# Regrouping y and z by batch: VectorE transposes in place of SBUF copies, in a linear-attention and spectral-mixing kernel

## The chip, the cores and the metric

The kernel runs on one core of a Trainium2 chip. The metric is the device time of one execution in microseconds (us). The core has TensorE (PE), VectorE (DVE), ScalarE (ACT), GpSimd (POOL) and SyncE (SP), which run side by side and wait for one another through semaphores; each takes its instructions in order. SP and POOL also issue DMA transfers, which sixteen DMA engines carry out.

## The reference

An attention with a feature map feeds a spectral mixing layer. Batch is 8, heads 8, sequence 576, head dimension 64; the model width is 512 and 64 Fourier modes are kept.

```python
q_p, k_p = (phi(q), phi(k))                       # exp(+-(x w_phi - max|x w_phi|))
kv = np.einsum('bhsf,bhsd->bhfd', k_p, v)
z = np.sum(k_p, axis=2)
x = num / den                                     # q_p kv / (q_p z + 1e-6), heads side by side
X = np.fft.rfft(x, axis=1)                        # first 64 modes
Yr = einsum('bmd,mde->bme', Xr, w_r) - einsum('bmd,mde->bme', Xi, w_i)
Yi = einsum('bmd,mde->bme', Xr, w_i) + einsum('bmd,mde->bme', Xi, w_r)
y = np.fft.irfft(Y, n=S, axis=1)
u = x + y
out = u + np.maximum(u @ w_ch, 0.0)
```

The weights w_r and w_i have 64 x 512 x 512 float32 values each, 64 MB each, and each is used once.

## The kernel before, in words

The model width is cut into four groups g of 128 rows (two heads each), and the 64 modes into eight *octets* o of eight modes. A weight tile is (g, 2 o + i): one octet, one group, i = 0 for w_r and 1 for w_i; 64 tiles of 1 MB in bf16. They stream from HBM in one fixed order (`order`), issued by POOL (`wload`, `next_w`), converted to bf16 on the way, into a pool `pw` of nine slots. The last eight tiles are those of octets 6 and 7 for g = 2 and 3.

**Unit loop.** 16 units (a group and a pair of batches, `bp`) run through a software pipeline: features, kv, numerators, the normalised x into `xs`, and its forward Fourier transform (`freq`, `keep_x`) into `XT`. In between, `some(n)` takes n weight tiles from `mixq` and *mixes* each: eight matmuls of 512 columns on TensorE (`mix`). The sum over groups lives in `yacc`, one slot of 128x512 float32 for each octet. At the end of the loop, in the pass after the last unit, three mixes are done.

**Late stage.** Then the loop `while mixq` mixes the rest: a mix, then n *fills* from the list `todo`, the number dealt out evenly over the mixes that are left. `left` is the number of tiles still to be mixed. `todo` holds, in this order: 36 chunks of channel work (`Channels`: transpose x on TensorE, copy to `xT` on VectorE, multiply with w_ch, copy to `xw` on ScalarE; `hold(i)` turns chunk i + 1 ahead of the product of chunk i), in whose first entries the inverse Fourier tables CI, CL, CM are built (`inverse_tables`, on VectorE and ScalarE); then the *sums* (`Absorb`): the inverse transform of y is added to x on VectorE and that of z = y w_ch to xw on ScalarE or GpSimd. The fills are dealt so that at `left == 8`, which is when tile (3, 11) was mixed, all but the last channel chunks are done; the sums run between the last eight mixes.

**One octet.** When an octet is summed over all groups (its last mix has g = 3 and i = 1), VectorE forms `yst` (128 partitions, 512 bf16), TensorE transposes it, VectorE and ScalarE copy that to `yT`, TensorE multiplies by w_ch, and the result is `zst`. In `yst` and `zst` a partition is a mode, a part and a batch together, and the columns are e. The sums need the modes on partitions and the batch in the columns. This regrouping is done by `put`, one DMA from SP for each of y and z of octets 0 to 6, into 16 partitions of `yall` and `zall`, which with `yl` are three of the nine slots of `pw`; row 16 o + r holds octet o. The sums then use the first 96 rows (112 for the six chunks that are summed last, `early`), as six (seven) octets are there. Octets 6 and 7 go to `yl` too, for the last pairs of chunks (`Pair`), which sum them with the table CL, or straight from `yst` and `zst` with CM.

**Tail.** The last mix completes octet 7. Behind it follow the 18 pairs of chunks: sums, the rectifier, the addition and the stores to HBM.

Each engine's order is the program's order, fixed by `InOrder`; nothing is rescheduled. Operations are recorded through that helper, so that the profile gives nearly all of them as line 37; the tile names tell them apart.

Of the kernel before, what the change touches and what calls it, by code (L numbers as in the profile page):

```python
# [19 lines left out]
DMODEL = 512  # L20
# [23 lines left out]
def kernel(  # L44
# [470 lines left out]
    for n in range(-2, len(units) + 1):  # L515
        P, Q, K, R = (unit(n + i) for i in (-1, 0, 1, 2))
        X = 0 if n < 4 else 6 if n == 4 else 3
        if Q:
            Q.exp_q(0)
        if K:  # L520
            K.rows_k(0)
            K.exp_k(0)
        if Q:
            Q.weigh_v2()
            if n + 3 == len(units):
                unit(n + 2).load_v_parts()
            elif unit(n + 2):
                unit(n + 2).load_v()
        if P:
            P.freq()  # L530
            assert not any(key[0] == P.g - 2 for key in mixq)
            P.keep_x()
            if P.bp == NP - 1:
                mixq += [key for key in order if key[0] == P.g and (P.g < 2 or key[1] < 12)]
        if Q:
            Q.cols_q(1)
            Q.exp_q(1)
        some(1 if X else 0)
        if K:
            K.rows_k(1)  # L540
            K.exp_k(1)
        if Q:
            Q.kv()
        some(2 if n == 4 else 0)
        if K:
            K.rows_q(0)
            K.rows_k(2)
            K.rows_q(2)
            K.rows_q(1)
        if Q:  # L550
            Q.cols_q(2)
            Q.keep_kv()
            Q.exp_q(2)
        if K:
            K.exp_k(2)
            K.weigh_v()
        some(1 if X else 0)
        if R:
            R.turn_k(0)
        if K:  # L560
            K.shift_q()
        if R:
            R.turn_k(1)
        if Q:
            Q.num(0)
        if K:
# [12 lines left out]
        some(X - 2 + (n == 12))  # L579
        if n == -1:  # L580
            forward_table()
        if n < 3:
            next_w((2, 3, 2, 3, 2)[n + 2])
        elif n == 3:
            next_w(1)
        if n == 6:
            pool.dma_start(wchb, moe_w_ch.rearrange("(dc p) e -> p dc e", p=128))
    mixq += order[-8:]
    pm_cm.__exit__(None, None, None)
    pin_cm.__exit__(None, None, None)  # L590
# [53 lines left out]
    def inverse_tables():  # L644

        flat = xw[:, NP - 1].rearrange("p n e -> p (n e)").bitcast(F32)
        tok, ang, rnd = (flat[:, 640 * i:640 * i + 640] for i in range(3))
        small = pb.tile([128, 40], F32, name="small", bufs=1)
        dve.tensor_copy(eye, ident_b)
        ints = pb.tile([128, 16], I32, name="ints", bufs=1)  # L650
        for c in range(4):
            for a in range(2):
                dve.tensor_scalar_add(
                    out=tok[:, 128 * c:128 * c + 128].rearrange("k (p a) -> k a p", a=2)[:, a],
                    in0=nine, scalar1=float(4 * a + c))
        for i in range(2):
            dve.tensor_scalar_add(out=tok[:, 512 + 64 * i:576 + 64 * i], in0=nine, scalar1=8.0)
        used = [0, 0]
        yield

        def bits(src, shift, mask):
            t, f = ints[:, used[0]:used[0] + 1], small[:, used[1]:used[1] + 1]
            used[0] += 1
            used[1] += 1
            dve.tensor_scalar(out=t, in0=src, scalar1=shift, scalar2=mask,
                              op0=ALU.logical_shift_right, op1=ALU.bitwise_and)
            dve.tensor_copy(f, t)
# [10 lines left out]
        mode = calc(bits(pi, 4, 7), 8.0, jt)  # L678
        late = calc(calc(bits(pi, 4, 1), 8.0, 48.0), 1.0, jt)
        jm, tm, rm, b = bits(pi, 5, 3), bits(pi, 4, 1), bits(pi, 3, 1), bits(pi, 0, 7)  # L680
        last = calc(calc(tm, 4.0, jm), 1.0, 56.0)
        only = [calc(b, float(i), 1.0, ALU.is_equal, ALU.mult) for i in range(2)]
        yield
        for dst, m, r in ((CI, mode, r), (CL, late, r), (CM, last, rm)):
# [24 lines left out]
            yield  # L709
# [118 lines left out]

    def fill(n):
        for _ in range(n):  # L830
            if todo:
                todo.pop(0)()

    def put(src, o, dst, copies):
        if o < 7:
            sp.dma_start(dst[16 * o:16 * o + 16], src)
        if o > 5:
            for s in copies:
                r = 32 * s + 16 * (o - 6)
                (pool if o == 6 or s == 3 else sp).dma_start(yl[r:r + 16], src)  # L840
# [113 lines left out]
    while mixq:  # L954
# [3 lines left out]
            next_w(1)  # L958
        if not mixq:
            assert not todo  # L960
            pe.matmul(pys[o], lhsT=eye, rhs=yacc[:, o, :], start=False, stop=False)
# [10 lines left out]
        if g == NG - 1 and i == 1:  # L972
# [8 lines left out]
            else:  # L981
                for h in range(2):
                    dve.tensor_tensor(out=yst[:, H * h:H * h + H], in0=py[:, H * h:H * h + H],
                                      in1=yacc[:, o, H * h:H * h + H], op=ALU.add)
            put(yst, o, yall, (0, 2))
            if o < 5:
                fill(min(n, 1))
            for h in range(2):
# [14 lines left out]
            for e in range(2):  # L1003
# [13 lines left out]
            put(zst, o, zall, (1, 3))  # L1017
            fill(max(n - 2, 0) if o < 5 else n)
        else:
            fill(n)  # L1020
# [34 lines left out]
```

## Time and profile before

| | |
|---|---|
| three runs | 437.73, 438.81, 440.0 us; median 438.81 |
| profiled execution: span from first to last instruction | 436.2 us |
| busy: PE, DVE, ACT, POOL | 328.4, 293.7, 290.3, 118.9 us |
| mean granted TensorE clock | 0.906 |
| HBM read, written | 163.64 MB, 9.44 MB |
| weight tiles, issue to landing (median) | 27.8 and 28.9 us |

The profiled execution's own time is known as its span; the median of the runs lies 2.6 us above it, which is what lies around the span, and the difference between runs.

In the lines of the profile, `out<-in` are tile names, a bracket at the end gives how long the engine had been idle before and who released it, and "x8" joins eight instructions in a row. Matmuls overlap: one of 512 columns is shown with 0.38 us, but starts 0.22 after the one before. VectorE's instructions overlap in the same way: 0.68 long, 0.60 apart.

### The profile page before, as it was taken

What the parts mean: (1) busy time and instruction counts of PE and PEld (TensorE: products, weight loads), DVE (VectorE), ACT (ScalarE), POOL (GpSimd) and SP (SyncE); (2) the same over time, 40 slices, a digit from 0 to 9 for tenths busy, and PEclk for the clock granted to TensorE, in tenths of its full rate; (3) what the DMA queues carried; (4) which work ended last, traced back from release to release, by engine and by line L of the source; (5) the groups of instructions that cost most, each with busy time, mean ns of one, the idle gap of its engine ahead of it and who ended that gap; (6) DMA issues with size and microseconds to landing.
All of it is one profiled execution on the core that took longest, in us unless ns stands there. A gap on an engine that the chain in (4) does not pass through costs nothing.

```text
span 436.2 us, 10104 instructions
## 1 busy us (share of the span) xinstructions
PE 328.4 (75%) x4205; PEld 196.4 (45%) x4205; DVE 293.7 (67%) x583; ACT 290.3 (67%) x472; POOL 118.9 (27%) x157
## 2 busy tenths in 40 slices
PE   1567667778697686787796877934679999998992
PEld 1345555555465454554564554611334554333320
DVE  6768687665786777887877778722783333885794
ACT  3788697786887977986977778600444442665871
POOL 6232132113221212222222121211101111483790
PEclk9779898789998989998987998875899999999998
DMA  9999999999999999999999999999999999998697
GB/s 213 209 211 210 238 212 237 235 215 241 235 211 239 218 230 238 238 210 239 223 225 238 211 258 215 213 211 212 212 215 223 219 224 222 212 218 182 232 391 293
DMA packets 51896, 99.55 MB, mean 228 GB/s; under 512 B 2538, under 2 KB 13546, under 8 KB 51850
## 3 DMA queue, kind: packets, MB, share of 16 engines
q0 software_dynamic: 45136, 85.40, 100.1%
q1 hardware_dynamic: 6554, 13.44, 8.7%
q8 instruction: 33, 0.54, 0.5%
q14 instruction: 13, 0.11, 0.1%
q10 hardware_dynamic: 160, 0.07, 0.1%
HBM read 163.64 MB, written 9.44 MB: 397 GB/s over the span
## 4 chain that ended last, share of the span: by engine, by line
ACT 28%; PE 25%; DMA 24%; DVE 12%; issue 7%; POOL 2%; DVEq 0%; POOLq 0%; ACTq 0%
DMA wt<-in_moe_w_r_dram 16%; PE one L37 13%; ACT AQ L37 13%; ACT AB L37 9%; PE two L37 8%; DMA wt<-in_moe_w_i_dram 8%; DVE m L37 6%; ACT qT L37 3%; ACT XT L37 3%; PE pp L37 2%; DVE mk L37 2%; PE pt L37 2%; DVE xs L37 1%; DVE yacc L37 1%; DVE of L37 1%
## 5 line engine op out<-in xcount | busy, mean ns | idle before, releaser
L37 ACT ACTIVATE AQ<-two 128x1024 bf16<-128x1024 f32 x64 | 80.5, 1347 | 2.9 <-PE two L37 2.8
L37 ACT ACTIVATE AB<-two 128x1024 bf16<-128x1024 f32 x64 | 62.9, 1058 | 2.9 <-DVE mk L37 2.7
L37 ACT CAST xw<-pt 128x512 bf16<-128x512 f32 x50 | 29.4, 587 | 48.0 <-PE pt L37 48.0
L37 DVE TENSOR_REDUCE m<-two 128x8 f32<-128x1024 f32 x32 | 39.1, 1223 | 20.8 <-PE two L37 20.8
L37 POOL DMA_DIRECT2D wt<-in_moe_w_i_dram x28 | 20.9, 748 | 95.2 <-PE pt L37 37.6
L37 DVE TENSOR_REDUCE mk<-two 128x8 f32<-128x1024 f32 x32 | 38.9, 1218 | 8.6 <-PE two L37 8.6
L37 PE MATMUL two<-w2blk,qT 128*128 128x256 bf16 x128 | 22.3, 303 | 27.1 <-ACT AQ L37 14.8
L37 DVE TENSOR_TENSOR va<-vn,ee 128x1152 bf16<-128x1152 f32 x32 | 42.0, 1354 | 0.0
L37 PE MATMUL pt<-wchb,xT 128*128 128x512 bf16 x136 | 36.8, 395 | 6.6 <-DVE xT L37 5.5
L37 POOL DMA_DIRECT2D wt<-in_moe_w_r_dram x30 | 22.3, 744 | 63.3 <-PE one L37 27.0
L37 PEld LDWEIGHTS <-xs 128*128 128x128 bf16 x624 | 31.6, 103 | 12.2 <-issue 6.4
L37 PE MATMUL one<-wt,XT 128*32 128x512 bf16 x304 | 27.3, 446 | 10.4 <-DMA wt<-in_moe_w_i_dram 4.6
L37 ACT COPY qT<-one 128x512 bf16<-128x512 bf16 (+1 forms) x32 | 19.0, 642 | 24.3 <-PE one L37 24.3
L37 PE MATMUL two<-qT,w2blk 128*128 128x512 bf16 x64 | 27.8, 435 | 9.5 <-ACT AQ L37 9.5
L37 PEld LDWEIGHTS <-qT 128*128 128x128 bf16 x144 | 14.7, 103 | 41.8 <-issue 38.6
L37 PEld LDWEIGHTS <-XT 128*32 128x32 bf16 x512 | 14.7, 149 | 34.9 <-issue 24.2
L37 PEld LDWEIGHTS <-AQ 128*128 128x128 bf16 x512 | 24.5, 108 | 7.6 <-issue 4.1
L37 DVE TENSOR_TENSOR xs<-one,rd 128x384 bf16<-128x384 f32 x48 | 26.8, 557 | 1.6
L37 PE MATMUL one<-kvz,AQ 128*128 128x65 bf16 x512 | 27.1, 208 | 0.9 <-ACT qT L37 0.8
L37 PE MATMUL two<-mT,minus 96*128 96x512 bf16 x64 | 27.8, 434 | 0.0
L37 POOL DMA_DIRECT2D kb<-in_k_dram x16 | 11.4, 712 | 58.2 <-PE one L37 52.0
L37 DVE COPY xT<-pt 128x512 bf16<-128x512 bf16 x36 | 15.2, 421 | 17.5 <-PE pt L37 17.5
(142 smaller groups left out, 711.7 us busy)
## 6 DMA issues: line engine op xcount, KB each, us to landing
wt<-in_moe_w_r_dram POOLq DMA_DIRECT2D x30, 1024.0 KB, 27.8
wt<-in_moe_w_i_dram POOLq DMA_DIRECT2D x28, 1024.0 KB, 28.9
out_dram<-of SPq DMA_DIRECT2D x15, 512.0 KB, 3.5
vn<-in_v_dram POOLq DMA_DIRECT2D x13, 576.0 KB, 25.0
kb<-in_k_dram POOLq DMA_DIRECT2D x16, 288.0 KB, 20.4
qb<-in_q_dram POOLq DMA_DIRECT2D x16, 288.0 KB, 19.2
xs<-in_moe_w_i_dram POOLq DMA_DIRECT2D x2, 1024.0 KB, 23.6
out_dram<-of SPq DMA_DIRECT2D x6, 256.0 KB, 2.9
```

The lines of the kernel that those rows point to most:

```text
L37: ins = f(*args, **kwargs)
```

## The change

The 14 DMA copies of `put` go (its copies to `yl` stay). In their place each octet 0 to 6 is *parked*: `park` is a VectorE transpose of 32x32 blocks of 4-byte words, from `yst` (or `zst`) into the octet's slot of `yacc`, which is no longer needed by then. And `lay(bp)` regroups, with two more transposes of 128x512 words, the slots of all octets into the columns of `yall` and `zall` of one pair of batches. At octet 5 `lay(3)` and `lay(0)` are called; 1 and 2 follow in `fill`, when a sum that needs them is near; `lay(0)` is called again at octet 6. A pair of bf16 values moves as one word.

So that all eight slots hold something finite, octets 6 and 7 of `yacc` are copied to a new tile `late` by ScalarE and set to zero by GpSimd; the adds and the float32 matmul that used them read `late`. The sums use all 128 rows. The table CI follows the new order of rows.

`yall`, `zall` and `yl` take their slots of `pw` later: at `left` 11, 10 and 6, and at the first two no tile is issued. In the last pass of the unit loop one tile is mixed and not three; two are left to the late stage.

```diff
@@ unit loop @@
-        some(1 if X else 0)
+        some(1 if X and not end else 0)
...
-        some(X - 2 + (n == 12))
+        some(0 if end else X - 2 + (n == 12))
@@ late stage @@
-    zall = pw.tile([128, B_, DMODEL], BF16, name="zall", tag="wt")
-    yall = pw.tile([128, B_, DMODEL], BF16, name="yall", tag="wt")
-    yl = pw.tile([128, B_, DMODEL], BF16, name="yl", tag="wt")
+    late = pb.tile([128, 2, DMODEL], F32, name="late", bufs=1)
+    act.copy(late, yacc[:, 6:8, :])
+    pool.memset(yacc[:, 6:8, :], 0.0)
+    slots = yacc.bitcast(I32)
...
-            self.rows = slice(0, 112 if self.early else 96)
+            self.rows = slice(0, 128)
...
     def fill(n):
         for _ in range(n):
+            for f in todo[:4] if laid else ():
+                c = getattr(f, "__self__", None)
+                if isinstance(c, Absorb) and c.bp not in laid:
+                    lay(c.bp)
...
-    def put(src, o, dst, copies):
-        if o < 7:
-            sp.dma_start(dst[16 * o:16 * o + 16], src)
+    def park(src, o, z):
+        dve.transpose(
+            out=slots[:, o, 256 * z:256 * z + 256].rearrange("p (b k x) -> p k x b", b=8, k=8),
+            in_=src.bitcast(I32).rearrange("p (k x b) -> p k x b", k=8, b=8))
+    def lay(bp):
+        for z, dst in enumerate((yall, zall)):
+            dve.transpose(
+                out=dst[:, 2 * bp:2 * bp + 2].rearrange("p b e -> p (b e)").bitcast(I32).rearrange(
+                    "p (c o x) -> p c o x", o=8, x=4),
+                in_=slots[:, :, 256 * z + 64 * bp:256 * z + 64 * bp + 64].rearrange(
+                    "p o (c x) -> p c o x", x=4))
+        laid.append(bp)
...
-        next_w(1)
         left = len(mixq)
+        if left == 11:
+            yall = pw.tile([128, B_, DMODEL], BF16, name="yall", tag="wt")
+        elif left == 10:
+            zall = pw.tile([128, B_, DMODEL], BF16, name="zall", tag="wt")
+        else:
+            next_w(1)
+        if left == 6:
+            yl = pw.tile([128, B_, DMODEL], BF16, name="yl", tag="wt")
...
                 else:
                     act.copy(yT[h], pt[h])
+            if o < 7:
+                park(yst, o, 0)
...
+            if o < 7:
+                park(zst, o, 1)
+            if o == 5:
+                lay(3)
+                lay(0)
+            elif o == 6:
+                lay(0)
             fill(max(n - 2, 0) if o < 5 else n)
```

More of the change, by code (lines that the diff above doesn't have):

```diff
@@ L517 @@
         X = 0 if n < 4 else 6 if n == 4 else 3
+        end = n == len(units)
         if Q:
@@ L587 @@
             pool.dma_start(wchb, moe_w_ch.rearrange("(dc p) e -> p dc e", p=128))
+    assert not pys
     mixq += order[-8:]
@@ L604 @@
     xw = pb.tile([128, NP, 9, DMODEL], BF16, name="xw", bufs=1)
-    zall = pw.tile([128, B_, DMODEL], BF16, name="zall", tag="wt")
-    yall = pw.tile([128, B_, DMODEL], BF16, name="yall", tag="wt")
-    yl = pw.tile([128, B_, DMODEL], BF16, name="yl", tag="wt")
+    late = pb.tile([128, 2, DMODEL], F32, name="late", bufs=1)
+    act.copy(late, yacc[:, 6:8, :])
+    pool.memset(yacc[:, 6:8, :], 0.0)
+    slots = yacc.bitcast(I32)
+    zall = yall = yl = None
     CI = pb.tile([128, 5, 128], BF16, name="CI", bufs=1)
@@ L677, in inverse_tables @@
         jt = calc(t, 4.0, j)
-        mode = calc(bits(pi, 4, 7), 8.0, jt)
-        late = calc(calc(bits(pi, 4, 1), 8.0, 48.0), 1.0, jt)
+        lm = calc(calc(bits(pi, 4, 1), 8.0, 48.0), 1.0, jt)
         jm, tm, rm, b = bits(pi, 5, 3), bits(pi, 4, 1), bits(pi, 3, 1), bits(pi, 0, 7)
+        mode = calc(bits(pi, 2, 7), 8.0, calc(t, 4.0, jm))
         last = calc(calc(tm, 4.0, jm), 1.0, 56.0)
@@ L683, in inverse_tables @@
         yield
-        for dst, m, r in ((CI, mode, r), (CL, late, r), (CM, last, rm)):
+        for dst, m, r in ((CI, mode, r), (CL, lm, r), (CM, last, rm)):
             n = 512 if dst is CM else 640
@@ L830, in fill, with put @@
         for _ in range(n):
+            for f in todo[:4] if laid else ():
+                c = getattr(f, "__self__", None)
+                if isinstance(c, Absorb) and c.bp not in laid:
+                    lay(c.bp)
             if todo:
                 todo.pop(0)()
-    def put(src, o, dst, copies):
-        if o < 7:
-            sp.dma_start(dst[16 * o:16 * o + 16], src)
+    def park(src, o, z):
+        dve.transpose(
+            out=slots[:, o, 256 * z:256 * z + 256].rearrange("p (b k x) -> p k x b", b=8, k=8),
+            in_=src.bitcast(I32).rearrange("p (k x b) -> p k x b", k=8, b=8))
+    laid = []
+    def lay(bp):
[6 more added lines that the diff above has]
+        laid.append(bp)
+    def put(src, o, z, copies):
         if o > 5:
@@ L960 @@
             assert not todo
-            pe.matmul(pys[o], lhsT=eye, rhs=yacc[:, o, :], start=False, stop=False)
+            pe.matmul(pys[o], lhsT=eye, rhs=late[:, o - 6], start=False, stop=False)
             until("mix")
         mix(*key, wts.pop(key), XTb[g % 2], bank)
-        next_w(1)
         left = len(mixq)
+        if left == 11:
[6 more added lines that the diff above has]
+            yl = pw.tile([128, B_, DMODEL], BF16, name="yl", tag="wt")
         if left > 8:
@@ L983 @@
                     dve.tensor_tensor(out=yst[:, H * h:H * h + H], in0=py[:, H * h:H * h + H],
-                                      in1=yacc[:, o, H * h:H * h + H], op=ALU.add)
-            put(yst, o, yall, (0, 2))
+                                      in1=(yacc[:, o] if o < 6 else late[:, o - 6])[:, H * h:H * h + H], op=ALU.add)
+            put(yst, o, 0, (0, 2))
             if o < 5:
@@ L1016 @@
                     act.copy(zst[:, cut[0]], pz[0])
-            put(zst, o, zall, (1, 3))
+            put(zst, o, 1, (1, 3))
+            if o < 7:
[4 more added lines that the diff above has]
+            elif o == 6:
+                assert all(f.__self__.early or f.__self__.bp for f in todo)
+                lay(0)
             fill(max(n - 2, 0) if o < 5 else n)
```

## The prediction

> **What bounds the kernel now.** I read the page first: engine shares, DMA row, DMA queues.
>
> ```profile
> span 436.2 us, 10104 instructions
> ...
> DMA  9999999999999999999999999999999999998697
> ...
> q0 software_dynamic: 45136, 85.40, 100.1%
> q1 hardware_dynamic: 6554, 13.44, 8.7%
> ...
> yall<-yst SPq DMA_DIRECT2D x7, 128.0 KB, 6.3
> zall<-zst SPq DMA_DIRECT2D x7, 128.0 KB, 6.5
> ```
>
> The DMA engines are full until about 400 us, and nearly all of it is q0, the weight stream. The 14 copies of y and z run beside it in q1. Second, the chain that ended last, in order of time: the last weight tile is issued at 367.54, lands 34.51 us later, and TensorE starts on it at once.
>
> ```profile
> 367.54 34.51 DMA wt<-in_moe_w_i_dram
> 402.05 0.04 issue
> 402.09 0.69 PE pt L37 x8
> ```
>
> Third, TensorE's timeline, for whether it could have been earlier.
>
> ```profile
> 291.59 1.08 PE L37 MATMUL one<-wt,XT 128*32 128x512 bf16 x8 [4.28 <-DMA wt<-in_moe_w_r_dram]
> 296.57 1.08 PE L37 MATMUL one<-wt,XT 128*32 128x512 bf16 x8 [3.90 <-DMA wt<-in_moe_w_i_dram]
> 301.53 1.08 PE L37 MATMUL pt<-wt,XT 128*32 128x512 bf16 x8 [3.88 <-DMA wt<-in_moe_w_r_dram]
> ...
> 361.41 0.66 PE L37 MATMUL pt<-wt,XT 128*32 128x512 bf16 x8
> ...
> 365.61 1.03 PE L37 MATMUL pt<-wchb,xT 128*128 128x512 bf16 x4
> ...
> 397.31 0.66 PE L37 MATMUL pt<-wt,XT 128*32 128x512 bf16 x8 [0.38 <-DMA wt<-in_moe_w_r_dram]
> ...
> 402.09 0.67 PE L37 MATMUL pt<-wt,XT 128*32 128x512 bf16 x8 [0.98 <-DMA wt<-in_moe_w_i_dram]
> ```
>
> Each line of eight matmuls is one mix. Up to 301.53 TensorE starves: a tile every 4.97 us ((301.53 - 291.59) / 2). From then to 397.31 no mix waits for a tile, and the last two wait only 0.38 and 0.98. So two chains end almost together at 402: the stream, and the late stage on TensorE and VectorE, 1.4 us behind at most. A faster stream alone buys 1.4 us; what counts is when the second chain starts and what is added to it.
>
> Fourth, VectorE where the change puts most of its work, and a wait of TensorE from the table building.
>
> ```profile
> 364.55 0.29 DVE L37 CAST zst<-pt 128x128 bf16<-128x128 f32 x1 [1.00 <-PE pt L37]
> 364.76 0.41 DVE L37 COPY xT<-pt 128x512 bf16<-128x512 bf16 x1
> ...
> 374.06 0.69 DVE L37 TENSOR_TENSOR xs<-pp,xs 128x512 bf16<-128x512 f32 x1 [1.55 <-PE pp L37]
> ```
>
> ```profile
> 313.02 1.78 PE L37 MATMUL pt<-wchb,xT 128*128 128x512 bf16 x4 [1.96 <-DVE xT L37]
> ```
>
> The xT copy at 364.76 feeds the product at 365.61. From 374 VectorE adds nearly back to back. And after a wait of 1.96 us a product took 1.78, where the usual is 1.03: the granted clock falls to half.
>
> **What the change removes.** 14 SP copies. From 301.53 to 402.09 nineteen tiles came, 5.29 us each, against 4.97 undisturbed: 0.32 x 19 = 6.1 us. This agrees with the queues: in a stretch with copies q0 fell from 112.0% to 101.7% while q1 took 10.0%. I take all 6.1: the last tile lands at 301.53 + 19 x 4.97 = 396.0. Bounds: 5.2 (1.84 MB of q1's 13.44 is 1.2% of 436) and 6.1. No starving threatens: loads were issued some 30 us ahead, and the three slots come out of the weight pool later than before. SP has only yl copies and stores behind these issues; nothing waits for it.
>
> **What it moves.** The mixes at 291.59 and 296.57, and the add of their octet into yacc, go from the unit loop into the late loop, so fills start behind the mix of 291.59, 10 us sooner. They cost TensorE about 0.66 + 0.42 of changeover each, VectorE one 0.69 add. But fills are dealt out per mix, with two mixes more, and mixes follow tiles. The decisive one is mix A, (3, 11), now at 361.41: all channel work but four chunks comes before it, and exactly the same work as before behind it. It is the eleventh tile after 301.53: 301.53 + 11 x 4.97 = 356.2. TensorE's work up to A: 361.41 - 301.53 = 59.9, without a tile wait, plus 2.2 and 0.7, from 291.6: 354.4. So the tile decides, 356.2 (bounds 354.4 and, if the table building starves TensorE more, 359): 5.2 us gained, not 10.
>
> From A to readiness for the last mix was 402.09 - 0.98 - 361.41 = 39.7, less the tile wait of 0.38: 39.3, TensorE-bound to 370 and VectorE-bound from 374.
>
> **What it adds.** No transpose is in this trace. Regrouping one tensor of one batch pair is 128x512 words of 4 bytes, parking an octet 128x256. Call L the spacing of the first, p of the second. Nearest row: the f32 add 128x512, 0.68 long, 0.605 apart; the 128x256 add of yst 0.42, 0.34 apart. I take L = 0.60, p = 0.35. Below: the one-source f32 row 128x512 (0.89 for two), L = 0.45, p = 0.25. Above: two cycles a word, like 1.22 for 128x1024, L = 1.2, p = 0.7.
>
> - Parks of octets 0 to 4, ten of 0.35: the next xT copy has over 1 us to its product, and VectorE is busy 11.71 of 31 us between 330 and 361. Nothing; 0.35 each without that cover.
> - Octet 5: the park of z waits for ScalarE's half of zst (about 364.9), then four L stand before the xT copy. Copy done at 364.93 + p + 0.1 + 4L + 0.42 = 368.2; its product at 365.61 moves 2.6 us (1.9 and 5.4 by the bounds), and all of TensorE's queue behind.
> - That idle 2.5 us is longer than the 1.96 that halved the clock: the product 1.78 for 1.03, the next z 1.91 for 1.04 and a turn 0.53 for 0.40, together 1.7. Waits of 1.24 and 1.37 had no such effect. By the nearest row I take 1.7; bounds 0 and 1.7.
> - Batch pair 1: 2L = 1.2 falls into the 1.55 idle at 374.06. Nothing (0.9 at the upper bound).
> - Batch pair 2: 2L less the 0.31 idle before octet 6's yst: 0.9 (0.6; 2.1).
> - Octet 6: p + 0.1 + 2L = 1.65 late on VectorE; its idle times from there to the end are 0.28, 0.22, 0.18 and 1.10, 1.8 in all. Nothing (0; 1.4).
> - ScalarE's copy of late (by the 128x512 f32 copy, 0.60, about 1.1) and GpSimd's memset stand near 288 to 290, where ScalarE does nothing until 302 and the loads behind the memset wait 4.2 us for a landing anyway. Nothing; at most 2 us on loads that run 30 ahead.
> - The 128 rows for 96 or 112 in the sums: rows on partitions; 112 rows cost 0.38 like 96. Nothing.
>
> The park writes words 128 bytes apart. [...] No row of this trace shows a VectorE write with such a stride.
>
> **Sum.** Last mix: 356.2 + 39.3 + 2.6 + 1.7 + 0.9 = 400.7, against 402.09: -1.4. The tail behind it (34.1 us of sums, stores and closing) is unchanged. The profiled span of 436.2 becomes 434.8. The median of the runs lies 2.6 above this span, and I leave that: 438.8 - 1.4 = 437.4.
>
> **Rivals.**
>
> 1. Cheaper regrouping, or a clock that holds. With L = 0.60 and no slowed clock: -3.1; with L = 0.45 as well: 356.2 + 39.3 + 1.9 + 0.6 = 398.0, -4.1, 434.7. It cannot pass the stream, 396.0. For it: a halved clock needs the wait to fall badly, and 1.37 was harmless. Against: 2.5 is well past 1.96.
> 2. Dear transposes: slower. Place: the four before octet 5's xT copy and the pair inside the add stage. Nothing lost up to additions of 402.09 - 356.2 - 39.3 = 6.6, which is L = 0.77 with the slowed clock; slower by over 0.5% (2.2 us, about what a measurement of this kernel can tell from no change) from L = 0.97. At L = 1.2: 5.4 + 1.7 + 0.9 + 2.1 + 1.4 = 11.5, +4.9, 443.7; at the middle, 1.05, about 442. For it: ScalarE's strided AQ (1347 ns) against AB (1058) is 1.27 times, which gives 0.77. Against: no VectorE row of one f32 source costs over 0.605 for 512.
> 3. TensorE, not the tile, sets mix A. If the longer table building and halved clock put A at 359, all is 2.8 later: +1.4, 440.2. For it: waits for xT of 0.96 to 1.96 between 308 and 324. Against: 1.8 us of margin.
>
> **How the numbers follow.** Forecast 0.42, rival 1 0.28, rival 2 0.22, rival 3 0.08. Of the forecast's 0.42, 0.12 lies beyond -2.2. Faster 0.28 + 0.12 = 0.40; same 0.30 + 0.06 = 0.36; slower 0.22 + 0.02 = 0.24. The range takes in rival 1's lower sum with a little of the stream's bound and rival 2 to L of about 1.0: 433.8 to 441.5. The forecast's own: 435.7 to 439.
>
> **What would show it.** Stream: no y and z issues by SP, last tile landed near 396 with its mix not waiting. Mix A near 356 behind a short tile wait. Ten transposes of 128x512 with mean near 0.69 and 0.60 apart; a wait of TensorE for xT of about 2.5 us behind octet 5's z and a half-speed stretch of the clock there. The last mix near 400.7. I am wrong if the transposes are over 0.9 apart, if that wait is hidden, or if the last mix again waits for its tile.

## The result, and the profile after

The changed kernel takes 436.56 us (median of 20 runs, 435.74 to 438.61); the kernel before takes 437.89 us (median of 20 runs, 437.26 to 440.00). The ratio is 0.997, with a 95% interval from 0.9957 to 0.9982: 1.3 us less (0.8 to 1.9). The forecast was 1.4 us less. The profiled execution of the changed kernel has a span of 435.1 us, against 436.2 before and 434.8 forecast.

The page of the changed kernel, span and DMA queues (packets, MB, share of sixteen engines):

```profile
span 435.1 us, 10067 instructions
...
DMA  9999999999999999999999999999999999993797
...
q0 software_dynamic: 45136, 85.40, 100.4%
q1 hardware_dynamic: 4538, 11.60, 7.1%
```

The copies are gone from q1 (13.44 MB before), and the DMA engines are busy for 3 tenths of slice 37, where it was 8 before. The stretches view around the end of the stream (columns: busy us of PE, PEld, DVE, ACT, POOL with instructions in parentheses, granted clock, share of the DMA engines, GB/s):

```profile
396.00:397.00 1.00, 1.00 (x6) 0.48 (x5) 0.99 (x3) 0.78 (x3) 0.71 (x1) 1.00 0.34 74
397.00:398.00 1.00, 1.00 (x11) 0.21 (x9) 0.96 (x2) 0.99 (x2) 0.44 (x1) 1.00 0.01 4
```

The last weight tile is in by 397, where before it landed at 402.05. TensorE's timeline (start, us, what, how long idle before and who ended it):

```profile
351.31 0.66 PE L37 MATMUL pt<-wt,XT 128*32 128x512 bf16 x8 [0.52 <-DMA wt<-in_moe_w_r_dram]
...
356.29 0.66 PE L37 MATMUL pt<-wt,XT 128*32 128x512 bf16 x8 [2.05 <-DMA wt<-in_moe_w_i_dram]
357.48 0.70 PE L37 MATMUL pt<-ident_b,yst 128*128 128x128 bf16 x4 [0.53 <-DVE yst L37]
358.29 1.89 PE L37 MATMUL pt<-wchb,yT 128*128 128x384 bf16 x8
...
363.89 1.04 PE L37 MATMUL pt<-wchb,xT 128*128 128x512 bf16 x4 [1.79 <-DVE xT L37]
...
387.05 0.38 PE L37 MATMUL pp<-yall,CI 128*128 128x512 bf16 x1 [1.31 <-ACT rl L37]
...
401.12 0.66 PE L37 MATMUL pt<-wt,XT 128*32 128x512 bf16 x8
```

Mix A stands at 356.29, behind a wait for its tile (361.41 before, with none). The last mix, at 401.12, waits for no tile any more: 4 us behind the stream, it ends a chain of work. From mix A to the last mix it is now 44.83 us; before it was 39.3 without the tile waits. So 5.12 us were gained ahead of mix A and 5.53 spent behind it. That the last mix comes 0.97 sooner all the same is the 1.36 us of tile waits (0.38 and 0.98) that the old kernel had there and the new one has not, less the 0.41. The tail is unchanged: 435.1 - 401.1 = 34.0.

What is spent begins on VectorE behind mix A. Its timeline, and the groups of the four kinds of transposes (total busy, mean ns of one, idle before):

```profile
360.61 0.62 DVE L37 STREAM_TRANSPOSE yacc<-zst 128x256 int32<-128x256 int32 x1
361.08 0.67 DVE L37 STREAM_TRANSPOSE yall<-yacc 128x512 int32<-128x512 int32 x1
361.67 0.67 DVE L37 STREAM_TRANSPOSE zall<-yacc 128x512 int32<-128x512 int32 x1
362.25 0.68 DVE L37 STREAM_TRANSPOSE yall<-yacc 128x512 int32<-128x512 int32 x1
362.85 0.68 DVE L37 STREAM_TRANSPOSE zall<-yacc 128x512 int32<-128x512 int32 x1
363.44 0.72 DVE L37 COPY xT<-pt 128x512 bf16<-128x512 bf16 x2
```

```profile
L37 DVE STREAM_TRANSPOSE yacc<-zst 128x256 int32<-128x256 int32 x7 | 4.4, 623 | 0.7
L37 DVE STREAM_TRANSPOSE yacc<-yst 128x256 int32<-128x256 int32 x7 | 4.3, 609 | 0.0
L37 DVE STREAM_TRANSPOSE yall<-yacc 128x512 int32<-128x512 int32 x5 | 3.4, 682 | 0.0
L37 DVE STREAM_TRANSPOSE zall<-yacc 128x512 int32<-128x512 int32 x5 | 3.3, 669 | 0.0
```

The regrouping transposes start 0.59 to 0.60 apart, as taken (L = 0.60). The parks are 0.61 long and 0.47 apart (361.08 - 360.61), where 0.35 was taken. The four in a row end at the xT copy of 363.44, and the product of 363.89 starts on it.

### The profile page after: what moved, and what is told of

Its sections match the earlier page's. It is cut to its first block, busy times and chain, and to the rows that moved or that the text cites. A ratio compares the mean times of both kernels' runs of the same rounds, so it can differ in the third digit from the quotient of the medians.

```text
span 435.1 us, 10067 instructions
## 1 busy us (share of the span) xinstructions
PE 328.3 (75%) x4205; PEld 196.1 (45%) x4205; DVE 306.7 (70%) x608; ACT 291.5 (67%) x473; POOL 120.2 (28%) x158
## 4 chain that ended last, share of the span: by engine, by line
PE 34%; ACT 26%; DMA 17%; DVE 17%; issue 4%; POOL 1%; ACTq 0%; DVEq 0%; POOLq 0%
PE one L37 13%; ACT AQ L37 11%; ACT AB L37 9%; PE pt L37 8%; DMA wt<-in_moe_w_i_dram 8%; DMA wt<-in_moe_w_r_dram 8%; PE two L37 8%; DVE m L37 5%; PE pp L37 4%; ACT XT L37 3%; ACT qT L37 2%; DVE xs L37 2%; DVE mk L37 2%; DVE of L37 1%; DVE xw L37 1%
## 5 line engine op out<-in xcount | busy, mean ns | idle before, releaser
L37 PE MATMUL pt<-wchb,xT 128*128 128x512 bf16 x136 | 38.1, 406 | 8.7 <-DVE xT L37 7.2
L37 POOL DMA_DIRECT2D kb<-in_k_dram x16 | 11.4, 714 | 56.8 <-PE one L37 49.4
L37 PE MATMUL one<-wt,XT 128*32 128x512 bf16 x288 | 24.7, 430 | 2.9 <-ACT XT L37 1.5
L37 DVE RECIPROCAL rd<-one 128x6 f32<-128x6 f32 x48 | 9.4, 195 | 23.7 <-PE one L37 23.4
```

What stands on the lines that cost most here:

```text
L37: ins = f(*args, **kwargs)
```

## The experiments

Two quantities are read from each profile: where mix A starts, and how long it is from there to the last mix. "A + 4.41" is 4.41 us behind the start of mix A. The tail behind is 33.6 to 34.4 us in all of them. Each ratio is to the kernel before, timed beside that run.

| run | mix A | to last mix | last mix | span | ratio to before (95%) |
|---|---|---|---|---|---|
| before | 361.41 | 40.68, of it 0.98 waiting | 402.09 | 436.2 | |
| after | 356.29 | 44.83 | 401.12 | 435.1 | 0.9970 (0.9957 to 0.9982) |
| e1_copies_back | 359.54 | 49.46 | 409.00 | 443.2 | 1.0147 (1.0130 to 1.0165) |
| e10_ten_copies | 360.46 | 46.50 | 406.96 | 441.4 | 1.0109 (1.0086 to 1.0131) |
| e2_mixes_unmoved | 362.42 | 44.00 | 406.42 | 440.4 | 1.0097 (1.0073 to 1.0120) |
| e3_mixes_moved_only | 360.32 | 41.90, of it 1.02 waiting | 402.22 | 435.9 | 1.0002 (0.9992 to 1.0013) |
| e4_lays_spread | 356.63 | 42.28 | 398.91 | 432.5 | 0.9927 (0.9908 to 0.9947) |
| e5_lays_twice | 356.86 | 49.47 | 406.33 | 440.2 | 1.0077 (1.0064 to 1.0089) |
| e6_chunk_later | 357.22 | 45.56 | 402.78 | 436.9 | 0.9984 (0.9973 to 0.9995) |
| e7_ten_more | 356.19 | 44.54 | 400.73 | 434.3 | 0.9999 (0.9986 to 1.0013) |
| e8_spread_later | 356.85 | 41.65 | 398.50 | 432.1 | 0.9918 (0.9901 to 0.9935) |
| e9_octet6_later | 356.76 | 43.61 | 400.37 | 434.2 | 0.9927 (0.9909 to 0.9945) |
| e11_octet6_none | 356.93 | 44.15 | 401.08 | 434.9 | 0.9951 (0.9933 to 0.9970) |
| e12_all_moved | 357.33 | 40.58 | 397.91 | 431.7 | 0.9911 (0.9889 to 0.9933) |

The theory was: the tile stream sets mix A, the moved mixes let TensorE be ready for it, and the transposes on VectorE, those of octet 5 above all, give most of the gain back behind it. The rivals: only one of the two, copies or mixes, matters; or VectorE is full anyway, so that it is all one where the transposes stand.

### The stream: copies put back beside the change

```diff
     eye = pb.tile([128, 128], F32, name="eye", bufs=1)
+    junk = pb.tile([128, 464], BF16, name="junk", bufs=1)
...
     def put(src, o, z, copies):
+        if o < 7:
+            sp.dma_start(junk, src[:, 0:464])
```

> The change, with 14 copies by SP put back beside it: each brings 464 of the 512 columns of y or z of octets 0 to 6 to a tile that nobody reads (nine tenths of the old bytes). The result stays the same; this is extra DMA work alone. My theory: the copies slow the weight stream as before, nine tenths of 6.1 us over the nineteen tiles, about 3.5 of it by the eleventh tile (11 x 0.32). Mix A moves from 356.3 to about 359.5 to 360, the last mix to about 404.5, and the time goes to 3 us above the changed kernel, +1.5 to +2.5 against the kernel before. Rival: the copies were free beside the stream and the gain came from moving two mixes; then mix A stays at 356.3 and the time is that of the changed kernel, -1.3 against the one before.

Mix A moved to 359.54, after 2.57 us of waiting for its tile, as the theory had it. But the time is 6.4 us above the kernel before and not 2, because of the experiment's own making. All copies write one tile, so each waits for the one ahead (6.2 us each), and octet 5's zst waited for its buffer. VectorE's timeline of this run:

```profile
366.00 0.29 DVE L37 CAST zst<-pt 128x128 bf16<-128x128 f32 x1 [3.69 <-DMA junk<-zst]
```

So only mix A is to be read from this run. The next puts ten copies back without that fault.

```diff
-    zall = yall = yl = None
+    zall = pw.tile([128, B_, DMODEL], BF16, name="zall", tag="wt")
+    yall = pw.tile([128, B_, DMODEL], BF16, name="yall", tag="wt")
+    yl = pw.tile([128, B_, DMODEL], BF16, name="yl", tag="wt")
...
     def put(src, o, z, copies):
+        if o < 5:
+            sp.dma_start((yall, zall)[z][16 * o:16 * o + 16], src)
...
-        if left == 11:
-            yall = pw.tile([128, B_, DMODEL], BF16, name="yall", tag="wt")
-        elif left == 10:
-            zall = pw.tile([128, B_, DMODEL], BF16, name="zall", tag="wt")
-        else:
-            next_w(1)
-        if left == 6:
-            yl = pw.tile([128, B_, DMODEL], BF16, name="yl", tag="wt")
+        next_w(1)
```

> The change, with ten of the fourteen copies back in their old form, those of octets 0 to 4, into the very slots of yall and zall, which are taken early as before (the transposes write over them later, and the result is the same). No copy waits for another's target, as they did in the run with all copies into one small tile. Theory: eight or nine of them fall before mix A and delay the stream by 3 to 4 us there; mix A moves from 356.3 to 359.5 to 360, the chain behind it stays at 43.8 to 45, the last mix comes at 403.5 to 405: +1.5 to +2.5 against the kernel before, +3 to +4 against the changed one. Rival: copies cost the stream nothing; then as the changed kernel.

TensorE's timeline of this run:

```profile
360.46 0.66 PE L37 MATMUL pt<-wt,XT 128*32 128x512 bf16 x8 [1.84 <-DMA wt<-in_moe_w_i_dram]
...
368.17 1.66 PE L37 MATMUL pt<-wchb,xT 128*128 128x512 bf16 x4 [2.07 <-DVE xT L37]
369.76 1.08 PE L37 MATMUL pt<-wt,XT 128*32 128x512 bf16 x8
...
376.15 0.66 PE L37 MATMUL pt<-wt,XT 128*32 128x512 bf16 x8
```

Mix A is 4.2 us later than in the changed kernel and again waits for its tile: the copies slow the stream, and the stream sets mix A. Their rival, that they cost nothing, is out. This run also takes the three slots early, as the kernel before did, so fewer are left for weight tiles; but the DMA engines are full in both, and between 320 and 356 us the weight queue moved 6.83 MB here, with 11.4% of the engines' time on q1 (before, 6.87 MB and 11.0%), and 7.59 MB in the changed kernel, with 111.9% on the weight queue and nothing on q1. In e1, where the slots are taken late, mix A is late too. The chain behind it is 1.7 us longer than after, of which nothing is a copy: the product of 368.17 comes at A + 7.71 (A + 7.60 after), but it takes 1.66 and the mix 1.08, for 1.04 and 0.66 after; 1.08 is what a mix took before at a granted clock of 0.50 (301.53). From that product to the second mix it is 7.98 us, against 6.43 after (370.32 - 363.89). This is why 4.8 us above the kernel before came out and not 2.

### The mixes: moved or not, alone

```diff
-        end = n == len(units)
+        end = False
```

> The change, but with all three mixes left in the last pass of the unit loop. My theory: fills then start 10 us later as before, mix A is set by TensorE's work behind 301.5 and stands at about 361.4 with no tile wait, although its tile has been there since 356; the added 5.5 us behind it put the last mix at 361.4 + 44.8 - 0.9 (no half clock at the wait for the tile of mix A) = about 405, so +3 against the kernel before and +4 against the changed one. Rival: only the end of the stream counts (396), the start of the fills does not; then the time is within 0.5 us of the changed kernel.

With all three mixes in the unit loop, mix A starts at 362.42 and waits for no tile, though with the same stream its tile came by 356.3 in the changed kernel; the chain behind is 44.00. The time is 4.2 us above the kernel before, more than the 3 expected, and mix A is 1.0 later than in that kernel. The clock does not explain this: it is at half until 306.55 here and until 306.35 before, and up to there the mixes are no more than 0.2 apart (307.20 against 307.02). Most of it arises while the tables are built. The park of a zst at 317.28 stands ahead of table work, which starts at 317.94 (316.93 before); the xT copy behind that comes at 320.39 (319.38), and TensorE waits 1.93 us for it where it waited 1.24. So the parks are not free where TensorE, and not the tile, sets mix A: this one cost 0.7. An earlier end of the stream does not bring mix A forward while the fills start as late as before: the theory's half holds.

```diff
@@ the kernel before @@
+        end = n == len(units)
...
-        some(1 if X else 0)
+        some(1 if X and not end else 0)
...
-        some(X - 2 + (n == 12))
+        some(0 if end else X - 2 + (n == 12))
```

> The kernel before, with nothing changed but that the two mixes move from the unit loop to the late stage (copies by SP stay, no transposes). My theory: mix A would be ready by TensorE at about 354 to 356 but its tile comes at 360 to 361, so it hardly moves (361.4 to about 360.7), and the last mix still waits for its tile, near 402: -0.5 to +0.3 against the kernel before. Rival: the earlier start of the fills is the whole gain; then mix A goes to about 356, and the time is 1.3 to 4 us lower.

TensorE's timeline:

```profile
360.32 0.66 PE L37 MATMUL pt<-wt,XT 128*32 128x512 bf16 x8 [1.77 <-DMA wt<-in_moe_w_i_dram]
...
402.22 0.66 PE L37 MATMUL pt<-wt,XT 128*32 128x512 bf16 x8 [1.02 <-DMA wt<-in_moe_w_i_dram]
```

Mix A now waits 1.77 us for a tile that copies make late, and the last mix still waits too: 1.0002, no change, as the theory said. So mix A needs both parts of the change: together they bring it 5.1 us sooner, the moved mixes alone 1.1, and the earlier stream with the mixes unmoved not at all. No run here leaves out the copies and adds no transposes, so what the stream alone would be worth at the end is not measured.

### The transposes of octet 5: spread, and doubled

```diff
         if i + 1 < len(ch):
             ch[i + 1].turn()
+            if pend:
+                bp, z = pend.pop(0)
+                lay(bp, (z,))
...
             if o == 5:
-                lay(3)
-                lay(0)
+                lay_later(3)
+                lay_later(0)
```

(`lay_later(bp)` puts the two transposes of `lay(bp)` into the list `pend`, from which each of the next four turns takes one, behind its xT copy.)

> The change, with the four regrouping transposes of octet 5 no longer in a row ahead of the xT copy, but one behind each of the next four xT copies. My theory: these four stand on TensorE's path with 2.4 to 2.6 us, and one at a time, behind the copy, each is hidden by the 1 us that an xT copy has in hand; the product behind mix A goes from A + 7.60 to about A + 5.2, the last mix to 398.5 to 399, the time 2 to 2.6 us below the changed kernel (-3.3 to -3.9 against the one before). Rival: VectorE is bound from there to the end of the adds, and the work only moves; then the time stays within 0.5 us of the changed kernel.

TensorE's and VectorE's timelines:

```profile
356.63 0.66 PE L37 MATMUL pt<-wt,XT 128*32 128x512 bf16 x8 [2.03 <-DMA wt<-in_moe_w_i_dram]
...
361.04 1.04 PE L37 MATMUL pt<-wchb,xT 128*128 128x512 bf16 x4
...
398.91 0.66 PE L37 MATMUL pt<-wt,XT 128*32 128x512 bf16 x8
```

```profile
360.58 0.40 DVE L37 COPY xT<-pt 128x512 bf16<-128x512 bf16 x1
360.90 0.67 DVE L37 STREAM_TRANSPOSE yall<-yacc 128x512 int32<-128x512 int32 x1
```

The product starts at A + 4.41, against A + 7.60 after and A + 4.20 before. The same transposes, one behind each copy, cost 0.2 us in place of 2.6. The time is 0.9927 of that before, 1.9 us below the changed kernel by the ratios, just short of the 2 to 2.6 expected. So their place was the cost, and VectorE was not full there: it was busy for 6.60 of 10.20 us from 356.1 to 366.3.

```diff
             if o == 5:
-                lay(3)
-                lay(0)
+                for bp in (3, 3, 0, 0):
+                    lay(bp)
```

> The change, with the four regrouping transposes at octet 5 done twice (eight in a row, same result). My theory: all of it stands ahead of the xT copy on TensorE's path, four more of 0.60 are 2.4 us, and the wait of TensorE goes from 1.79 to 4.2, which may halve the clock for another 3.4 us of window (1.5 us more): 2.4 to 3.9 us above the changed kernel. Rival: later idle time of VectorE and TensorE takes it up; under 1 us.

```profile
366.94 1.89 PE L37 MATMUL pt<-wchb,xT 128*128 128x512 bf16 x4 [4.46 <-DVE xT L37]
368.75 1.08 PE L37 MATMUL pt<-wt,XT 128*32 128x512 bf16 x8
```

In TensorE's timeline above the product stands at A + 10.08, 2.48 later than after: four transposes of 0.60 and nothing else. Behind it product and mix run at half the clock (granted 0.50), and it is 8.59 us from the product to the second mix (375.53), 2.16 more than after. Together 4.64, the whole difference of the chains. The time is 0.0107 above the changed kernel by the ratios, 4.7 us; expected were 2.4 to 3.9, with one more halved stretch of 3.4 us where two came (364.8 to 371.6).

### The clock: one chunk of channel work moved

```diff
         if left > 8:
-            n = -(-max(len(todo) - A - 2, 0) // (left - 8))
+            n = 3 if left > 16 or left == 9 else 2
```

> The change, with the fills dealt so that one chunk of channel work moves from ahead of the mix before A to just ahead of mix A. Nothing is added. My theory now: TensorE's waits for tiles before A (0.52 and 2.05 us) get shorter, the longest to 1 us or less, since its work is the same; the half-clock stretch at 358 to 361.5 (product 1.89 for 1.04) comes from the 2.05 wait and goes with it, the chain behind mix A gets 1 to 1.5 us shorter, the time 0.9 to 1.5 below the changed kernel. Rival: the half clock follows the waits for xT (the lays), as I had forecast; then it stays and the time is the same within 0.3.

The edit takes the chunk from further ahead than the expectation says: in the changed kernel three stand between the mixes at 322.6 and 328.1, in this run two. The expectation failed: the ratio is 0.9984, 0.6 us above the changed kernel, which the two intervals do not tell from no change. In every trace here the granted clock changes only at borders 3.41 us apart (3.413 on average before and after); the stretch between two of them is called a slot below, and a slow slot is one at half clock (granted 0.50). TensorE's timeline, and the stretches view of this run cut at these borders (columns as above; the last but two is the granted clock):

```profile
357.22 0.66 PE L37 MATMUL pt<-wt,XT 128*32 128x512 bf16 x8 [0.94 <-DMA wt<-in_moe_w_i_dram]
...
363.98 1.41 PE L37 MATMUL pt<-wchb,xT 128*128 128x512 bf16 x4 [2.40 <-DVE xT L37]
365.32 1.08 PE L37 MATMUL pt<-wt,XT 128*32 128x512 bf16 x8
```

```profile
357.70:361.10 3.40, 2.63 (x24) 1.47 (x21) 2.27 (x6) 0.85 (x2) 0.00 (x0) 1.00 1.12 209
361.10:364.50 3.40, 1.00 (x9) 0.49 (x7) 3.16 (x7) 0.59 (x1) 0.00 (x0) 1.00 1.12 213
364.50:367.90 3.40, 3.18 (x17) 1.10 (x17) 0.42 (x1) 0.59 (x1) 0.74 (x1) 0.50 1.12 213
```

The tile wait did shrink, to 0.94, and the slow slot behind it went. But then zst came earlier, TensorE waited the full 2.40 us for the transposes, and the clock was halved behind that wait: the place that the prediction had named. Yet a wait of that length does not halve the clock by itself. In e2 TensorE waits as long for the same copy:

```profile
369.19 1.04 PE L37 MATMUL pt<-wchb,xT 128*128 128x512 bf16 x4 [2.41 <-DVE xT L37]
```

There a border at 367.99 cuts the wait in two, TensorE is busy for 2.2 us in each of the two slots, and the clock stays full: this product takes 1.04 and the mix behind it 0.67. In e6 the whole wait lies in one slot, with TensorE busy for 1.0 us of it. The same view of the changed kernel, cut 0.2 us behind its borders (354.46, 357.88, 361.29), and of the run with the transposes spread:

```profile
354.70:358.10 3.40, 1.24 (x12) 0.44 (x11) 0.76 (x2) 0.41 (x2) 0.00 (x0) 0.97 1.12 211
358.10:361.50 3.40, 3.29 (x17) 1.85 (x17) 2.00 (x5) 0.61 (x2) 0.00 (x0) 0.53 1.13 212
361.50:364.90 3.40, 1.61 (x14) 0.66 (x14) 2.66 (x6) 0.59 (x1) 0.00 (x0) 1.00 1.12 211
```

```profile
352.70:356.10 3.40, 1.90 (x12) 0.94 (x11) 0.83 (x2) 1.17 (x2) 0.18 (x1) 1.00 1.11 208
356.10:359.50 3.40, 2.11 (x20) 1.05 (x20) 1.58 (x4) 0.39 (x2) 0.00 (x0) 1.00 1.12 212
```

Both have the same tile wait, 2.05 and 2.03 us, at the same place. In the changed kernel 1.8 us of it fall into one slot, TensorE is busy for 1.0 us of that slot (1.24 in the stretch as cut here), and the next slot is at half clock. In the other the wait is cut in two by a border, TensorE is busy for 1.90 and 2.11, and the clock stays. So the length of a wait alone does not decide; how busy TensorE was within a slot counts (1.0 us in the two slots here that a slow one followed, 1.90 to 2.2 in the four that none followed), and with it where the slots lie.

The run also prices the transposes alone: up to the product the clock is full in it, and the product stands at A + 6.76, so 2.56 above the A + 4.20 of before. The remaining 0.84 to the A + 7.60 of the changed kernel is the slow slot of 358 to 361.3. e2 bears out both: the product stands at A + 6.77, no slot behind mix A is slow, and the chain is 44.00, 0.83 shorter than in the changed kernel.

### Both of these, as a candidate

The edits of e4 and e6 together.

> The change, with both: the four transposes of octet 5 one behind each of four xT copies, and the chunk moved to just ahead of mix A. My theory: the two gains add up, as one is a wait for xT behind mix A and the other a clock slowed by the tile wait ahead of it: 2.9 to 4 us below the changed kernel, the last mix at 397 to 398, within 2 us of the end of the stream at 396, which is the floor. Rival: both remove the same delay, or the add stage of VectorE takes over as the bound: no more than the better of the two alone, 2 to 2.5 below.

The ratio is 0.9918, 2.3 us below the changed kernel where 2.9 to 4 were expected, and the chain is 41.65: no slot of it is slow (granted clock 1.00 from 355 to 398). That is 0.63 shorter than with the spread alone, which had one slow slot in octet 6 (0.52 from 379.8 to 383.2). In times the two can't be told apart (0.9918 and 0.9927, intervals overlapping). The better of the two alone is about what came, so the rival had the size right: the moved chunk by itself is worth nothing that can be measured.

### Ten more transposes among the parks

```diff
     eye = pb.tile([128, 128], F32, name="eye", bufs=1)
+    junk = pb.tile([128, 224], I32, name="junk", bufs=1)
...
+        if o < 5:
+            dve.transpose(out=junk, in_=src.bitcast(I32)[:, 0:224])
```

(at the end of `park`)

> The change, with ten more transposes of 128x224 words, contiguous on both sides, from yst and zst of octets 0 to 4 to a tile that nobody reads, each behind the park of the same tile. It measures two things. Cost: my theory has the parks of octets 0 to 4 hidden, so ten more of about 0.3 cost nothing (within 0.4 us of the changed kernel); the rival, that VectorE's work before mix A counts in full, gives +2.5 to +3. Size: a contiguous transpose of 128x224 would take 0.37 us by an add of 128x256 (0.42 long); if the park's writes 128 bytes apart cost nothing extra it takes 0.53, as the park (0.61) by its words.

The group of the added transposes behind yst in this run:

```profile
L37 DVE STREAM_TRANSPOSE junk<-yst 128x224 int32<-128x224 int32 x5 | 1.8, 368 | 0.0
```

The contiguous one is 0.37 long, as an add of its size; by its words the park would be 0.42, and it is 0.61 as in the changed kernel. With its writes 128 bytes apart it is 1.45 times as long as that. As to the cost, the profile has it hidden: mix A at 356.19, the chain 44.54. But that execution was the fastest of its kernel; by the ratios the kernel is 1.3 us above the changed one (0.5 to 2 by the two intervals taken together), with runs from 436.28 to 440.56. That is more than the 0.4 of the theory and less than the 2.5 to 3 of the rival. No trace shows one of the longer executions, so it stays open what they lose and where.

### Octet 6: left out, and deferred

```diff
             elif o == 6:
...
-                lay(0)
+                pass
```

> The change, without the pair of regrouping transposes at octet 6 (the last sums of one pair of batches then lack octet 6; nothing else differs). It prices that pair alone, which I had forecast at nothing. Theory now: its 1.2 us and the 1.31 wait of TensorE go, 1.2 to 1.5 us below the changed kernel, -2.5 to -2.8 against the one before. As forecast: no difference from the changed kernel.

TensorE's timelines of this run and of the changed kernel, the mixes on both sides of octet 6:

```profile
381.40 0.66 PE L37 MATMUL pt<-wt,XT 128*32 128x512 bf16 x8
...
388.67 0.66 PE L37 MATMUL pt<-wt,XT 128*32 128x512 bf16 x8
```

```profile
380.27 0.66 PE L37 MATMUL pt<-wt,XT 128*32 128x512 bf16 x8
...
388.71 0.66 PE L37 MATMUL pt<-wt,XT 128*32 128x512 bf16 x8
```

7.27 us against 8.44: the pair costs 1.17, and the 1.31 wait for ScalarE's copy is gone. What made that wait, by the timelines of VectorE and ScalarE in the changed kernel:

```profile
385.08 0.66 DVE L37 STREAM_TRANSPOSE zall<-yacc 128x512 int32<-128x512 int32 x1
385.67 0.65 DVE L37 TENSOR_TENSOR xs<-pp,xs 128x512 bf16<-128x512 f32 x1
386.41 0.59 ACT L37 COPY rl<-pp 128x512 f32<-128x512 f32 x1 [2.54 <-DVE xs L37]
```

The add stands behind the pair, the copy behind the add: the copy starts 6.14 us after the mix, and 4.98 in this run. The time is 0.9951, 0.8 us below the changed kernel and not 1.2 to 1.5, and the intervals overlap. In the profiled execution two slow slots behind mix A (357.1 to 363.9, granted clock 0.50) cost 1.3 us (9.06 to the next mix, 7.73 in e2).

```diff
             elif o == 6:
...
-                lay(0)
+                laid.remove(0)
```

(on top of e4; the look-ahead in `fill` then calls `lay(0)` when a sum that needs it is three away)

> As the run with the four transposes of octet 5 spread, and besides the pair of regrouping transposes of octet 6 is not made at once but where the first sum that needs octet 6 is three sums ahead. Theory from the trace after: that pair makes VectorE's adds late, ScalarE's copies of pp wait for them and TensorE waits 1.31 us for the copy; deferred, the wait goes and the last mix comes 0.6 to 1.3 us sooner than in the run with the spread alone (a chain from mix A of 41 to 41.7 us in place of 42.28), -3.8 to -4.4 against the kernel before. Rival: VectorE is full from there to the end, the pair costs its 1.2 us wherever it stands; then there is no difference.

Octet 6 again takes 7.27 us (379.98 to 387.25), but the deferred pair makes a later stretch longer: 391.56 to 396.65 is 5.09, where it was 4.40 after. So 0.7 of the 1.17 is lost again there. This is near the rival: behind octet 6 VectorE is nearly full (after, busy for 7.35 of 8.00 us from 390 to 398). The chain is 43.61 and not 41 to 41.7, because two slow slots behind mix A (357.0 to 363.8: yT's product takes 1.89 and the next xT's 1.91, for 1.05 and 1.03 in e4) make it 7.81 to the next mix, for 5.38 in e4; without them it would be 41.2. The time, 0.9927, is that of the spread alone, where 3.8 to 4.4 us below the kernel before were expected and 3.2 came.

### All transposes in places of their own

On top of e9: the pair of batch pair 1 behind the last xT copy, that of batch pair 2 where pair 1's was.

```diff
         ch[i].hold(ab[i].q)
+        if i == K + 2:
+            while pend:
+                bp, z = pend.pop(0)
+                lay(bp, (z,))
...
-                if isinstance(c, Absorb) and c.bp not in laid:
-                    lay(c.bp)
+                if isinstance(c, Absorb):
+                    for bp in (c.bp, 2):
+                        if bp not in laid and (c.bp == bp or c.bp == 1):
+                            lay(bp)
...
                 lay_later(0)
+                lay_later(1)
```

> A candidate for the best: the spread of octet 5's four transposes, octet 6's pair deferred, and besides the pair of batch pair 1 made behind the last xT copy (VectorE has 0.9 us idle there) and that of batch pair 2 in the place of pair 1's (1.5 us idle). Theory: pair 2's 0.8 us come back as well, the chain from mix A is 40 to 41 us, the last mix 396.3 to 397.5, at or just behind the end of the stream at 396: -4.5 to -5.5 against the kernel before. Rival: the add stage of VectorE is full and gives nothing; then as the run with octet 6 deferred.

The chain is 40.58, the shortest with transposes, and the last mix at 397.91 (mix A came 1 us later in this execution than after, with its tile). Batch pair 2's pair costs nothing now: the mixes around it are 5.18 and 6.95 apart, 5.63 and 7.27 in e9, so 0.77 is gained. The time is 0.9911, the lowest here, 2.6 us below the changed kernel and 3.9 below the one before, where 4.5 to 5.5 were expected; against e8 and e4 it can't be told apart. The floor is the stream: in this execution the DMA engines fall from a share of 0.63 to 0.30 between 396 and 398, so the chain ends with it to about 1 us.

## Why the prediction was right, step by step

- **Stream and mix A.** Forecast 356.2, set by the tile; measured 356.29 behind a tile wait of 2.05; TensorE was ready at 354.24, forecast 354.4. The copies put back (359.54, 360.46) and the mixes moved back (362.42, no tile wait) show both conditions. The stream's end was forecast at 396.0 and lies before 397.
- **Octet 5.** Forecast 2.6 for park and four transposes ahead of the xT copy; 2.56 measured with the clock full (e6; 2.57 in e2), and 2.48 for four more (e5).
- **The slowed clock.** Forecast 1.7, behind the wait for xT. In the profiled execution it cost 0.84 and stood elsewhere, behind the tile wait at mix A. The step that failed is "by the nearest row I take 1.7": it took the length of the wait for the cause. The wait for xT was 1.79 there and did nothing (clock 1.00 behind it); in e6 it was 2.40 and cost 1.55 (7.98 from product to second mix, for 6.43), in e2 it was 2.41 and cost nothing. So the size was right for the place named, but whether the clock falls there, at mix A or in neither place goes by the position of the slots.
- **Batch pairs 1 and 2.** Pair 1: forecast nothing, and the mixes around it are 4.32 apart, 4.33 before. Pair 2: forecast 0.9; 0.77.
- **Octet 6.** Forecast nothing, since 1.65 late on VectorE met 1.8 us of idle to the end. Measured 1.17 for the pair; another 0.34 is left when the pair is not there (6.95 between the mixes in e12, 6.61 before), and nothing but the octet's two parks is added there. What failed is the comparison with all idle to the end: in the changed kernel ScalarE's copy of a pp tile waited 2.54 for VectorE's add from the same tile, and TensorE's next sum 1.31 for that copy. TensorE lost these 1.31 at once, while its own work behind was as long as VectorE's; idle on VectorE later on doesn't give that back.
- **Parks.** 0.47 apart, 0.35 taken. Those of octets 0 to 4 were forecast at nothing, and nothing of them shows in the changed kernel, where mix A waits 2.05 us for its tile in any case. In e2, where it waits for none, one of them cost 0.7 during the table work. The prediction's reason, over 1 us in hand for the next xT copy, was read from 330 to 361 us, which is behind the table work. The park, with its writes 128 bytes apart, is 0.61 long, for the 0.42 that e7's contiguous transposes give for its size.
- **Sum.** 356.29 + 39.3 + 2.56 + 0.84 + 0.77 + 1.17 + 0.34 = 401.3, measured 401.12; the last two stretches between mixes are 0.17 shorter than before without their tile waits. Forecast 400.7: the clock taken too high by 0.9 and octet 6 too low by 1.5 cancel in the main. The change of -1.4 was thus right to 0.1 us in part by luck, and the measured interval is itself 1.1 us wide. By the prediction's own line of 0.5% the change counts as none, to which it gave 0.36; it gave faster 0.40.
- **The level.** Forecast 437.4, measured 436.56. The 438.81 of the three runs was high by 0.9 against the later median of 437.89.

Rival 1 (cheaper, or a clock that holds) had the right idea of the clock, which holds in some executions, but without octet 6. Rival 2 is out with L = 0.60, rival 3 with a tile wait of 2.05 at mix A.

## What to carry to other kernels

A bundle of short operations that the engine could hide one by one becomes a wait when it stands in one place (here a park and four transposes in a row cost 2.56 us, with the four one by one 0.2): count the slack behind each instruction that another engine waits for, and put one piece into each. When one chain is shortened, look at once for the one close behind it (here 1.4 us), and shorten both or neither. Lateness on an engine is to be compared with the slack of those who wait for it, not with its own idle time to the end.

## What the runs showed of the hardware

The granted clock steps only at borders 3.41 us apart, 3.413 on average before and after; their position against the start of the kernel differs from execution to execution (306.35 before, 306.68 after). The fourteen traces (before, after, twelve experiments) were cut into these slots, from 17 to 422 us. All 140 slots in which TensorE was busy for under 40% were followed by one at half clock, 68 of 90 between 40 and 50%, 7 of 106 between 50 and 60%, and none of 746 over 90%; between 60 and 90% it was 74 of 555, most of them in the unit loop with its small matmuls, so busy time is not the whole measure. Before and after alone it was, in the same order, 22 of 22, 10 of 13, 1 of 12, none of 114 and 7 of 73. In the changed kernel 1.8 us of a wait of 2.05, with another 0.53 in the same slot, left TensorE busy for 1.0 of 3.41 us, and the next slot was at half clock. One slow slot cost 0.55 us (e7, 8.28 from mix A to the next mix for 7.73 in e2) to 1.55 us (e6) in the chain, as large as the change's whole gain, and timed executions of one kernel differ by up to 4.3 us (e7). That these differences between executions come from the slots is argued, not shown: only the profiled executions have traces.
